# Issuing all q and k transposes of a group ahead of their two PSUM copies, and loading the first V later, in a chunked attention followed by a squared-ReLU FFN

## The chip, the cores and the metric

The kernel runs on one NeuronCore of a Trainium2 chip. TensorE multiplies and transposes into PSUM, VectorE and ScalarE empty PSUM and do the elementwise work, GpSimd casts the weights to bf16, and SyncE issues every transfer between HBM and SBUF, in the order of the program. The metric is the device time of one execution in microseconds, lower being better.

## What is computed

Attention within chunks of 64 positions, over 8 batches, 8 heads, 576 positions and a head dimension of 64, and then a two-layer FFN over the 4608 tokens.

```python
scores = scale * np.matmul(q_c, k_c.transpose(0, 1, 2, 4, 3))    # per chunk of 64
attn = np.exp(scores - max)
attn = attn / (np.sum(attn, axis=-1, keepdims=True) + 1e-09)
x = np.matmul(attn, v_c)              # -> tokens x 512
h = np.maximum(x @ w_in, 0.0)         # 512 -> 2048
out = h * h @ w_out                   # 2048 -> 512
```

## The kernel before

The 4608 tokens are cut into 18 groups of 256 (two tiles of 128 tokens, `t` or `i` in the code), and the groups into blocks: groups 0 to 2, then seven pairs (3 and 4, up to 15 and 16), and group 17 alone. A block is the unit of the FFN; the attention of the next block's groups is woven into it.

The attention of a group has four steps. `transpose_qk` (T, line 129) takes the upper bf16 half of the fp32 q and k tiles and transposes them on TensorE, 8 transposes of 128 x 128 for q and 8 for k (line 139). They go into one PSUM tile `ps_att` of two banks, q in the first and k in the second. VectorE copies the q half to the SBUF tile `qkT` (line 146), ScalarE the k half (line 148). In the program the q transposes come first, then the q copy, then the k transposes, then the k copy. `scores` (SC, line 150) multiplies the chunks from `qkT` into another `ps_att` tile, and ScalarE takes the exponential (line 167). `values` (AV, line 170) multiplies with V, which has a column of ones that gives the sums, and VectorE divides (lines 186 and 189). `transpose_x` (XT, line 195) transposes the result into `xT`, with a copy on VectorE (line 209). `ps_att` has two buffers for all these steps.

The FFN of a block goes in slots. A slot of `ffn_in` (line 217) is one of 16 columns of tiles: 4 matmuls into a `ps_ffn` buffer (line 224), a relu on ScalarE (line 230) and a square on VectorE (line 231). A slot of `ffn_out` (line 235) is 4 of the 16 matmuls of an output tile (line 240); behind the last of them stand ScalarE's copy to `o_sb` (line 247, four buffers) and the store (line 249). `ps_ffn` has four buffers, so that slot n of `ffn_in` needs the buffer that the relu of slot n - 4 (or an output copy) has read.

The order is written out by hand (`manual_schedule`): each engine works through its instructions in the order of the program. The steps T, SC, AV, XT of groups 0 and 1 run ahead of everything, one after the other. In block 0, T of group 2 stands behind slot 3, and those of groups 3 and 4 behind slots 44 and 46, in its `ffn_out`. In the blocks that follow, T of the next pair stands behind slots 1 and 4 of `ffn_in`, the scores of both behind slot 9, the values behind 14 and 18, the last transposes behind 22 and 26.

The loads are issued by SyncE in a fixed order: q,k and then V of group 0, the same of group 1, two of the eight pieces of w_in (256 columns each, cast by GpSimd at line 113, each good for two slots), group 2, the other pieces of w_in, w_out, and the groups of the next two blocks; later ones at the start of each block, ahead of the stores of that block. `load_qk` (line 77) issues 4 transfers, or more where a batch ends within the group; `load_v` (line 90) issues 6 or more, as V is stored with its odd heads in swapped chunks.

Of the kernel before, what the change touches and what calls it, by code (L numbers as in the profile page):

```python
# [10 lines left out]
BF16 = mybir.dt.bfloat16  # L11
# [5 lines left out]
def kernel(  # L17
# [16 lines left out]
    n_hp = H // 2  # L34
    n_dt = d_model // 128
    n_ft = d_ff // 128
    GT = 256
# [8 lines left out]
    att_pool = ctx.enter_context(tc.tile_pool(name="att", bufs=3))  # L46
# [20 lines left out]
    def segments(g0, n):  # L67
        while n:
            b, s = divmod(g0, S)
            m = min(n, S - s)  # L70
            yield b, s, m
            g0 += m
            n -= m
# [3 lines left out]
    def load_qk(g):  # L77
        q_sb = in_pool.tile([128, 2, H, D], FP32, name="q_sb")
        k_sb = in_pool.tile([128, 2, H, D], FP32, name="k_sb")
        qk[g] = (q_sb, k_sb)  # L80
        for t in range(2):
            for dst, src in ((q_sb, q), (k_sb, k)):
                p = 0
                for b, s, m in segments(g * GT + t * 128, 128):
                    nc.sync.dma_start(  # L85
                        out=dst[p:p + m, t, :, :],
                        in_=src[b, :, s:s + m, :].rearrange("h s d -> s h d"))
                    p += m

    def load_v(g):  # L90

        vt = v_tiles[g % NV]
        for t in range(2):
            g0 = g * GT + t * 128
            p = 0
            for b, s, m in segments(g0, 128):
                nc.sync.dma_start(  # L97
                    out=vt[p:p + m, t, 0::2, 0:D],
                    in_=v[b, 0::2, s:s + m, :].rearrange("h s d -> s h d"))
                p += m  # L100
            for half in range(2):
                b, s = divmod(g0 + 64 * half, S)
                p = 64 * (1 - half)
                nc.sync.dma_start(  # L104
                    out=vt[p:p + 64, t, 1::2, 0:D],
                    in_=v[b, 1::2, s:s + 64, :].rearrange("h s d -> s h d"))

    def load_w_in(i):
        cols = slice(i * 256, (i + 1) * 256)
        st = wst_pool.tile([128, 1024], FP32, name="w_st").rearrange("p (a f) -> p a f", a=n_dt)  # L110
        nc.sync.dma_start(  # L111
            out=st, in_=moe_w_in[:, cols].rearrange("(a p) f -> p a f", p=128))
        nc.gpsimd.tensor_copy(out=w_in_bf[:, :, cols], in_=st)  # L113
# [15 lines left out]
    def transpose_qk(g):  # L129
        ps = ps_att.tile([128, 1024], FP32, name="ps_att")  # L130
        psb = ps.bitcast(BF16)
        qkT = att_pool.tile([128, 2, n_hp, GT], BF16, name="qkT")
        state["qkT", g] = qkT
        for which in range(2):
            srcb = qk[g][which].bitcast(BF16)
            for hp in range(n_hp):
                for i in range(2):
                    c0 = which * 1024 + hp * GT + i * 128
                    nc.tensor.transpose(  # L139
                        out=psb[:, c0:c0 + 128],  # L140
                        in_=srcb[:, i, 2 * hp:2 * hp + 2, 1::2],
                        identity=ident)
            dst = qkT[:, which]
            src = psb[:, which * 1024:(which + 1) * 1024].rearrange("c (h t) -> c h t", h=n_hp)
            if which == 0:
                nc.vector.tensor_copy(out=dst, in_=src)  # L146
            else:
                nc.scalar.copy(out=dst, in_=src)  # L148

    def scores(g):  # L150
        qkT = state.pop(("qkT", g))
        ps = ps_att.tile([128, 1024], FP32, name="ps_att")
        for hp in range(n_hp):
            for t in range(2):
                for a in range(2):
                    for p in range(2):
                        c = p ^ a
                        cols = slice(t * 128 + p * 64, t * 128 + p * 64 + 64)
                        o0 = a * 512 + hp * 128 + t * 64
                        nc.tensor.matmul(  # L160
                            out=ps[64 * c:64 * c + 64, o0:o0 + 64],
                            lhsT=qkT[64 * a:64 * a + 64, 1, hp, cols],
                            rhs=qkT[64 * a:64 * a + 64, 0, hp, cols],
                            start=True, stop=True)
        e = att_pool.tile([128, 2, n_hp, 2, 64], BF16, name="e")
        state["e", g] = e
        nc.scalar.activation(  # L167
            out=e.rearrange("p a h t q -> p (a h t q)"), in_=ps, func=AF.Exp, scale=scale)
# [26 lines left out]
    def transpose_x(g):  # L195
# [5 lines left out]
        for t in range(2):  # L201
# [9 lines left out]
            in_=psb[:, 0:1024].rearrange("p (h t) -> p h t", h=n_hp))  # L211

    T, SC, AV, XT = transpose_qk, scores, values, transpose_x

    gTs = {}
# [37 lines left out]
    def load(g):  # L253
        load_qk(g)
        load_v(g)

    load(0)
    load(1)
    load_w_in(0)
    load_w_in(1)  # L260
    load(2)
    for i in range(2, 8):
# [10 lines left out]
    for j, grps in enumerate(blocks):  # L273
# [4 lines left out]
        if j == 0:  # L278
            a, b = nxt
# [4 lines left out]
        else:  # L284
            if len(nxt) == 2:
                a, b = nxt
                plan = {1: [(T, a)], 4: [(T, b)], 9: [(SC, a), (SC, b)], 14: [(AV, a)],
                        18: [(AV, b)], 22: [(XT, a)], 26: [(XT, b)]}
            elif nxt:
                a, = nxt  # L290
# [40 lines left out]
```

## Time and profile before

| | us |
|---|---|
| time, median of 3 runs | 353.45 (352.02 to 353.71) |
| the profiled execution, its own time | 352.24 |
| its span, from the first to the last instruction | 350.2 |
| TensorE busy, of the span | 303.3 |
| TensorE's wait in the middle of T, all groups | 23.9 |
| VectorE, ScalarE, GpSimd busy | 120.7, 142.7, 18.6 |

The profile is that of one execution. A page sums up each engine's busy time; views of the trace list the waits of each engine with what ended them, the instructions in order of time, the chain of work that ended last, and the busy time by stretch. L139 is line 139 of the kernel before. PE is TensorE, PEld its weight load, DVE VectorE, ACT ScalarE, POOL GpSimd, SPq the queue from which SyncE issues transfers.

### The profile page before, as it was taken

How to read it: one execution, taken by the hardware profiler on the slowest of the kernel's cores; microseconds unless marked ns; L12 is line 12 of the kernel's file. 1: busy time of each engine (PE TensorE's matmuls, PEld its weight loads, DVE VectorE, ACT ScalarE, POOL GpSimd, SP SyncE). 2: the span in 40 equal slices, each digit the busy share in tenths (PEclk: the TensorE clock that was granted, in tenths of full speed). 3: DMA queues.
4: the chain of work that ended last, by engine and by line, in shares of the span. 5: the costliest groups of instructions: out<-in, count | busy, mean ns of one | idle time of the engine just before them, and what ended most of it. 6: DMA issues, size and time to landing. Idle time of an engine off the chain costs nothing.

```text
span 350.2 us, 6792 instructions
## 1 busy us (share of the span) xinstructions
PE 303.3 (87%) x2800; PEld 157.9 (45%) x2800; DVE 120.7 (34%) x268; ACT 142.7 (41%) x233; POOL 18.6 (5%) x28
## 2 busy tenths in 40 slices
PE   2456979989589988998899889988998899899995
PEld 1322447444244544454445444544454445444472
DVE  0322395015235314531453145314531453144050
ACT  0323545250455146514651465146514651473171
POOL 1021681000000000000000000000000000000000
PEclk9999899999699999999999999999999999999999
DMA  9997998998992159414861586159615601100101
GB/s 168 193 229 217 366 362 179 200 172 172 278 187 48 60 140 199 85 62 117 183 122 62 135 168 121 63 136 171 115 62 138 104 2 60 62 0 31 60 32 60
DMA packets 125278, 46.58 MB, mean 133 GB/s; under 512 B 114496, under 2 KB 118592, under 8 KB 125248
## 3 DMA queue, kind: packets, MB, share of 16 engines
q1 hardware_dynamic: 125248, 46.15, 56.9%
q8 instruction: 22, 0.36, 0.5%
q14 instruction: 8, 0.07, 0.1%
HBM read 36.70 MB, written 9.44 MB: 132 GB/s over the span
## 4 chain that ended last, share of the span: by engine, by line
PE 78%; SPq 8%; DVE 6%; ACT 3%; DMA 2%; issue 1%; POOL 0%; ACTq 0%
PE ps_ffn L240 36%; PE ps_ffn L224 35%; SPq L85 3%; PE ps_att L139 3%; DVE gT L231 3%; DVE qkT L146 3%; ACT rl L230 3%; SPq L104 2%; PE ps_att L205 2%; SPq L97 2%; PE ps_att L179 2%; PE ps_att L160 2%; DMA w_st<-in_moe_w_in_dram 1%; DMA out_dram<-o_sb 1%; SPq L111 1%
## 5 line engine op out<-in xcount | busy, mean ns | idle before, releaser
L224 PE MATMUL ps_ffn<-xT,w_in_bf 128*128 128x512 bf16 (+1 forms) x640 | 137.5, 369 | 6.1 <-DVE xT L209 4.0
L240 PE MATMUL ps_ffn<-w_out_bf,gT 128*128 128x512 bf16 x576 | 130.0, 379 | 0.0
L231 DVE TENSOR_TENSOR gT<-rl 128x512 bf16<-128x512 bf16 (+1 forms) x160 | 68.0, 428 | 136.2 <-ACT rl L230 131.6
L230 ACT ACTIVATE rl<-ps_ffn 128x512 bf16<-128x512 f32 (+1 forms) x160 | 87.5, 557 | 45.2 <-PE ps_ffn L224 42.7
L224 PEld LDWEIGHTS <-w_in_bf 128*128 128x128 bf16 x640 | 62.0, 100 | 66.1 <-issue 8.8
L240 PEld LDWEIGHTS <-gT 128*128 128x128 bf16 x576 | 55.0, 98 | 62.0
L247 ACT COPY o_sb<-ps_ffn 128x512 f32<-128x512 f32 x36 | 21.1, 586 | 113.4 <-PE ps_ffn L240 103.7
L139 PE MATMUL ps_att<-ident,k_sb 128*128 128x128 bf16 x144 | 12.2, 233 | 23.9 <-DVE qkT L146 23.9
L148 ACT COPY qkT<-ps_att 128x1024 bf16<-128x1024 bf16 x18 | 18.2, 1012 | 35.5 <-PE ps_att L139 35.5
L209 DVE COPY xT<-ps_att 128x1024 bf16<-128x1024 bf16 x18 | 12.4, 691 | 38.7 <-PE ps_att L205 38.7
L189 DVE TENSOR_TENSOR x<-ps_att,rec 128x512 bf16<-128x512 f32 x36 | 24.9, 692 | 1.2
L139 PEld LDWEIGHTS <-k_sb 128*128 128x128 bf16 x144 | 10.5, 104 | 26.3 <-issue 15.7
L146 DVE COPY qkT<-ps_att 128x1024 bf16<-128x1024 bf16 x18 | 12.3, 686 | 21.4 <-PE ps_att L139 21.4
L167 ACT ACTIVATE e<-ps_att 128x1024 bf16<-128x1024 f32 x18 | 17.6, 1023 | 2.1 <-PE ps_att L160 2.1
L139 PE MATMUL ps_att<-ident,q_sb 128*128 128x128 bf16 x144 | 12.0, 229 | 6.2 <-DMA q_sb<-in_q_dram 6.2
L139 PEld LDWEIGHTS <-q_sb 128*128 128x128 bf16 x144 | 10.2, 103 | 10.3 <-DMA q_sb<-in_q_dram 6.3
L186 DVE RECIPROCAL rec<-ps_att 128x8 f32<-128x8 f32 x36 | 7.2, 201 | 22.0 <-PE ps_att L179 22.0
L205 PE MATMUL ps_att<-ident,x 128*128 128x128 bf16 x144 | 12.2, 229 | 2.2 <-DVE x L189 2.2
L205 PEld LDWEIGHTS <-x 128*128 128x128 bf16 x144 | 9.9, 101 | 6.8 <-DVE x L189 3.0
L179 PEld LDWEIGHTS <-e 64*64 64x64 bf16 x576 | 6.5, 111 | 9.3 <-issue 5.5
L179 PE MATMUL ps_att<-v_sb,e 64*64 64x65 bf16 x576 | 8.6, 200 | 2.3 <-ACT e L167 2.3
L113 POOL CAST w_in_bf<-w_st 128x1024 bf16<-128x1024 f32 x8 | 8.8, 1096 | 32.7 <-DMA w_st<-in_moe_w_in_dram 32.7
(12 smaller groups left out, 24.6 us busy)
## 6 DMA issues: line engine op xcount, KB each, us to landing
out_dram<-o_sb SPq DMA_DIRECT2D x36, 256.0 KB, 2.0
q_sb<-in_q_dram SPq DMA_DIRECT2D x32, 256.0 KB, 4.3
k_sb<-in_k_dram SPq DMA_DIRECT2D x32, 256.0 KB, 4.8
v_sb<-in_v_dram SPq DMA_DIRECT2D x80, 64.0 KB, 3.0
v_sb<-in_v_dram SPq DMA_DIRECT2D x32, 128.0 KB, 4.5
w_st<-in_moe_w_in_dram SPq DMA_DIRECT2D x8, 512.0 KB, 5.7
w_st<-in_moe_w_out_dram SPq DMA_DIRECT2D x8, 512.0 KB, 6.3
q_sb<-in_q_dram SPq DMA_DIRECT2D x8, 128.0 KB, 3.6
```

Of the source, the lines that this page charges most:

```text
L139: nc.tensor.transpose(out=psb[:, c0:c0 + 128], in_=srcb[:, i, 2 * hp:2 * hp + 2, 1::2], identity=ident)
L146: nc.vector.tensor_copy(out=dst, in_=src)
L148: nc.scalar.copy(out=dst, in_=src)
L167: nc.scalar.activation(out=e.rearrange("p a h t q -> p (a h t q)"), in_=ps, func=AF.Exp, scale=scale)
L179: nc.tensor.matmul(out=ps[64 * p:64 * p + 64, a, hp * (D + 1):(hp + 1) * (D + 1)], lhsT=e[64 * c:64 * c + 64, a, hp, t, :], rhs=vb[64 * c: ...
L189: nc.vector.tensor_tensor(out=x.rearrange("p h a d -> p a h d"), in0=o[:, :, :, 0:D], in1=rec.to_broadcast([128, 2, n_hp, D]), op=ALU.mult)
L205: nc.tensor.transpose(out=psb[:, c0:c0 + 128], in_=x[:, hp].rearrange("p a d -> p (a d)"), identity=ident)
L224: nc.tensor.matmul(out=h[:, 0:n], lhsT=w_in_bf[:, dt, ft * 128:(ft + 1) * 128], rhs=xT[:, dt, c:c + n], start=(dt == 0), stop=(dt == n_dt ...
L230: nc.scalar.activation(out=rl[:, 0:n], in_=h[:, 0:n], func=AF.Relu)
L231: nc.vector.tensor_tensor(out=gT[:, ft, c:c + n], in0=rl[:, 0:n], in1=rl[:, 0:n], op=ALU.mult)
L240: nc.tensor.matmul(out=o_ps, lhsT=gT[:, ft, tt * 128:(tt + 1) * 128], rhs=w_out_bf[:, ft, :], start=(ft == 0), stop=(ft == n_ft - 1))
L247: nc.scalar.copy(out=o_sb, in_=o_ps)
```

## The change

All 16 transposes of a group are issued first, q and then k, and the two copies after them. Within each half the PSUM columns and the `qkT` tile are ordered by token tile first and head pair second, instead of the other way round, and the scores' slices follow; every run that an instruction reads or writes stays 64, 128 or 1024 elements long. In the loads, q,k of groups 0 and 1 come first, then V of group 0, w_in 0, V of group 1, w_in 1; from group 2 on the order is the same as before.

```diff
@@ transpose_qk
-        qkT = att_pool.tile([128, 2, n_hp, GT], BF16, name="qkT")
+        qkT = att_pool.tile([128, 2, 2, n_hp, 128], BF16, name="qkT")
         state["qkT", g] = qkT
         for which in range(2):
             srcb = qk[g][which].bitcast(BF16)
             for hp in range(n_hp):
                 for i in range(2):
-                    c0 = which * 1024 + hp * GT + i * 128
+                    c0 = which * 1024 + i * 512 + hp * 128
                     nc.tensor.transpose(
                         out=psb[:, c0:c0 + 128],
                         in_=srcb[:, i, 2 * hp:2 * hp + 2, 1::2],
                         identity=ident)
-            dst = qkT[:, which]
-            src = psb[:, which * 1024:(which + 1) * 1024].rearrange("c (h t) -> c h t", h=n_hp)
+        for which in range(2):
+            dst = qkT[:, which].rearrange("c t h q -> c (t h q)")
+            src = psb[:, which * 1024:(which + 1) * 1024]
             if which == 0:
                 nc.vector.tensor_copy(out=dst, in_=src)
             else:
@@ scores
-                        cols = slice(t * 128 + p * 64, t * 128 + p * 64 + 64)
+                        cols = slice(p * 64, p * 64 + 64)
...
-                            lhsT=qkT[64 * a:64 * a + 64, 1, hp, cols],
-                            rhs=qkT[64 * a:64 * a + 64, 0, hp, cols],
+                            lhsT=qkT[64 * a:64 * a + 64, 1, t, hp, cols],
+                            rhs=qkT[64 * a:64 * a + 64, 0, t, hp, cols],
@@ loads
-    load(0)
-    load(1)
+    load_qk(0)
+    load_qk(1)
+    load_v(0)
     load_w_in(0)
+    load_v(1)
     load_w_in(1)
     load(2)
```

## Rows read from the trace of the kernel before

**Rows 1.** The page, busy time of each engine, share of the span, instructions.

```profile
PE 303.3 (87%) x2800; PEld 157.9 (45%) x2800; DVE 120.7 (34%) x268; ACT 142.7 (41%) x233; POOL 18.6 (5%) x28
```

**Rows 2.** The waits: who waited for whom, us in total, times, longest.

```profile
PE ps_att L139 <- DVE qkT L146: 23.9, 18, 3.5
```

**Rows 3.** Stretches: us, busy time by engine, PEclk, DMA share, GB/s; a steady block.

```profile
126.03:161.05 35.02, 32.36 (x306) 16.32 (x304) 12.62 (x28) 15.29 (x24) 0.00 (x0) 1.00 0.57 121
```

**Rows 4.** Timeline of a steady block: start, duration, instruction, [idle before <- releaser].

```profile
197.62 0.61 PE L139 MATMUL ps_att<-ident,q_sb 128*128 128x128 bf16 x8
...
198.79 0.68 DVE L146 COPY qkT<-ps_att 128x1024 bf16<-128x1024 bf16 x1
...
199.53 0.61 PE L139 MATMUL ps_att<-ident,k_sb 128*128 128x128 bf16 x8 [1.30 <-DVE qkT L146]
...
200.17 1.01 ACT L148 COPY qkT<-ps_att 128x1024 bf16<-128x1024 bf16 x1 [1.76 <-PE ps_att L139]
...
204.53 0.61 PE L139 MATMUL ps_att<-ident,k_sb 128*128 128x128 bf16 x8 [1.36 <-DVE qkT L146]
...
209.39 0.71 PE L160 MATMUL ps_att<-qkT 64*64 64x64 bf16 x64
```

**Rows 5.** Timeline from the end of block 0 into block 1.

```profile
70.44 0.61 PE L139 MATMUL ps_att<-ident,k_sb 128*128 128x128 bf16 x8 [0.78 <-DVE qkT L146]
...
85.71 4.20 SPq L249 DMA_DIRECT2D out_dram<-o_sb  x6
...
88.17 0.59 ACT L247 COPY o_sb<-ps_ffn 128x512 f32<-128x512 f32 x1 [9.46 <-PE ps_att L139]
88.97 0.59 ACT L247 COPY o_sb<-ps_ffn 128x512 f32<-128x512 f32 x1 [0.21 <-DMA out_dram<-o_sb]
...
91.65 1.01 PE L139 MATMUL ps_att<-ident,k_sb 128*128 128x128 bf16 x8 [3.54 <-DVE qkT L146]
...
92.46 5.18 PE L224 MATMUL ps_ffn<-xT,w_in_bf 128*128 128x512 bf16 x12
...
104.35 0.71 PE L160 MATMUL ps_att<-qkT 64*64 64x64 bf16 x64
...
106.76 1.63 ACT L230 ACTIVATE rl<-ps_ffn 128x512 bf16<-128x512 f32 x3
```

**Rows 6.** Timeline of the start: loads, groups 0 to 2, the first FFN slots.

```profile
3.73 1.08 SPq L97 DMA_DIRECT2D v_sb<-in_v_dram  x1
...
10.67 0.93 SPq L85 DMA_DIRECT2D k_sb<-in_k_dram  x1
...
12.31 0.66 PE L179 MATMUL ps_att<-v_sb,e 64*64 64x65 bf16 x32 [1.13 <-ACT e L167]
...
24.57 5.83 PE L224 MATMUL ps_ffn<-xT,w_in_bf 128*128 128x512 bf16 x16 [0.78 <-DVE xT L209]
...
33.74 1.04 POOL L113 CAST w_in_bf<-w_st 128x1024 bf16<-128x1024 f32 x1 [9.24 <-DMA w_st<-in_moe_w_in_dram]
...
34.84 4.27 PE L224 MATMUL ps_ffn<-xT,w_in_bf 128*128 128x512 bf16 x12 [2.07 <-POOL w_in_bf L113]
```

**Rows 7.** The k copy's line: ScalarE's queue, ns min/median/max, first and last start.

```profile
L148 ACTq EVENT_SEMAPHORE  x18: 17/17/17, 8.1 to 304.6; - x18
```

**Rows 8.** Timeline of group 17, the last q copy.

```profile
303.87 0.68 DVE L146 COPY qkT<-ps_att 128x1024 bf16<-128x1024 bf16 x1
```

**Rows 9.** The chain of work that ended last: start, us, engine, tile, line.

```profile
69.21 0.46 PE ps_att L139 x8
...
135.12 4.32 PE ps_ffn L224 x20
```

**Rows 10.** Stretches with the granted clock (the third column from the end).

```profile
90.50:91.00 0.50, 0.00 (x0) 0.00 (x0) 0.44 (x3) 0.04 (x1) 0.00 (x0) 0.54 1.07 320
...
47.50:51.00 3.50, 1.08 (x7) 0.36 (x5) 3.50 (x5) 1.20 (x2) 3.02 (x3) 1.00 1.02 378
```

**Rows 11.** Issues of V's line 104 up to 36 us.

```profile
DMA to landing us min/median/max: 2.7/3.6/4.5
```

## The prediction

> **What bounds the kernel now.** I read the page's busy shares first: TensorE is busy 87% of the span and no other engine over 45% [rows 1], so what matters is where TensorE stands still. The view of waits puts the largest sum of its waits on line 139: 23.9 us in 18 waits for VectorE's copy of line 146, one for each group [rows 2]. The table by stretches then shows how much that is of a steady block of two groups: 35.02 us, of which TensorE is busy 32.36 [rows 3]. The timeline of such a block has the missing 2.66 us as two gaps and nothing else: the 8 q transposes end, TensorE waits 1.30 us (in the block's second group 1.36) until the q copy is done, and only then come the 8 k transposes [rows 4]. The 18 waits are 0.78 us in groups 0, 1, 3 and 4 (one row stands for them), 1.30 in group 2, 3.54 in group 5, 1.36 in group 6, 1.30 and 1.36 in the five pairs of groups 7 to 16, and 1.30 in group 17; together 23.9 [rows 2, 4, 5].
>
> Before about 92 us the bound is another one. The chip's transfers run almost without a pause from the start, and TensorE meets two gates that SyncE's queue sets: the third piece of w_in, whose cast ends at 34.78, with the matmuls that need it at 34.84 [rows 6], and the first two stores of the output, issued from 85.71 on, behind every load of groups 3 to 6; ScalarE's copies of the fifth and sixth output tile (there are four o_sb buffers) wait for them until 88.17 and 88.97 [rows 5]. What TensorE wins ahead of a gate is lost at it.
>
> **The change part by part.**
>
> *Transposes ahead of the copies.* Same 16 transposes, same two copies, same bytes; the four edits of layout only reorder columns in runs that stay contiguous, so I cost them at nothing (copies of 0.68 and 1.01 us either way [rows 4]). What goes is TensorE's wait between the two halves. What is late next? The ScalarE queue has a semaphore step ahead of each of the 18 k copies, the first at 8.1 and the last at 304.6, when the last q copy (303.87, 0.68 long) has just ended; so the k copy waits for the q copy [rows 7, 8]. I take that to stay. Then the relus of the next slots, queued on ScalarE behind the k copy, hold ps_ffn buffers that TensorE wants four slots later. Worked through in a steady block: a slot is 4 matmuls of 0.216 (20 in 4.32) = 0.86 us, 16 transposes are twice 0.46 = 0.9 us, a relu is 0.54 us in a row of them (3 in 1.63) [rows 4, 5, 9]. T of the first group runs 197.62 to 198.52. The q copy starts at 198.79 as before (VectorE is busy until then), ends 199.47; the k copy runs 199.55 to 200.5, relus of slots 2 to 4 follow. T of the second group: 201.10 to 202.00; its q copy stands behind the square of slot 4 and ends at 203.23, the k copy at 204.22; the relu of slot 5 ends at 204.82. TensorE reaches slot 9, which needs that buffer, at 205.45: 0.63 us to spare. The scores come at 206.3 with the k copy two microseconds old, against 209.39 before; the k copy's own two releases of the rotating ps_att buffers are as early. So nothing takes the wait's place, and a steady block gains 2.66 us: five blocks 13.3 us, group 17 another 1.3. Behind the waiting k copy stand only relus; behind the q copy, which now waits for the k transposes too, only squares, and it was not ready to start sooner.
>
> *Groups 0 to 4.* In groups 0 and 1 nothing else is at hand for TensorE, and the chain transposes, q copy, k copy, scores keeps its length: 0 us. Group 2's 1.30 us ends at the gate of 34.84: 0. The 0.78 us of groups 3 and 4 bring TensorE to block 1 1.56 us sooner, and the gate of the stores takes it: 0.
>
> *Groups 5 and 6.* Here the old wait was 3.54 us because the q copy stood behind squares, relus and the two output copies that the stores held. After: slots 0 and 1 and all 16 transposes end at about 87 (91.65 less 3.54 is 88.11; less 1.56, plus 0.45 for the k half); slot 2 needs the buffer that the output copy at 88.17 (0.59 long) frees, so it starts at 88.82 instead of 92.46. The clock decides the rest. Before, it was granted 0.54 in the half microsecond from 90.5, after 2.4 us of standing still, and the 12 matmuls that began at 92.46 took 5.18 us instead of 2.6 [rows 5, 10]. Now the idle stretch is about 1.9 us; one of 2.4 us before 50.83 passed at full clock [rows 10]. At full clock slots 2 to 4, T of group 6 and slots 5 to 8 end at 95.8, slot 9 waits 1.1 us for ScalarE (relus 2 to 4 and the k copies start late here), and the scores come at 97.8 instead of 104.35: 6.5 us won, of which 4.9 are the old waits. With a fall to half clock it is some 4.5 to 5. I take 6.0, nearer the row that held its clock.
>
> *V behind q,k.* No transfer is added. In SyncE's queue the 6 of V of group 0 move behind 4 of group 1's q,k, and V of group 1 behind w_in 0, whose cast comes sooner on an idle GpSimd. All the bytes of the two groups are then issued by the same time as before, so w_in 2 and everything later keeps its time. But V of group 0 was issued from 3.73; now its last piece takes the place that the last k of group 1 had, 10.67 to 11.6 [rows 6], or about 12 since six short issues cost more than the rate of the transfers. With 2.7 to 3.6 us to landing [rows 11] it is there at 14.3 to 15.6. The values matmuls ran at 12.31 [rows 6], so they start 2 to 3.3 us late (q,k half of that chain is late too: the q copy now waits for the k data and the table load comes after it). TensorE takes groups in order, so the first FFN matmul, 24.57, goes to about 27.3. Its 16 matmuls took 5.83 us (33.1), T of group 2 one (34.1): still ahead of 34.84, by 0.7 us. Cost 0, ends 0 and +2.
>
> The Trainium skill speaks against this part: "DMA: Bandwidth & Descriptors", Rules for kernel authors, wants a transfer issued early and waited for late. By that rule the 3 us would stand in the result (334.6); the trace's gate at 34.84 says they don't.
>
> **Sum.** 13.3 + 1.3 + 6.0 = 20.6 us off the profiled execution's own 352.24 (span 350.2 and 2.04 around it, unchanged): 331.6. That execution lies near the low end of the three runs, whose median is 353.45, so I add 0.4: **332.0 us**.
>
> **Rivals.**
> 1. *ScalarE holds the buffers.* The margin of 0.63 us at slot 9 is thin. If the two copies, now behind each other with no wait of TensorE beside them, cost twice as long, the relu of slot 5 is 1.7 us late and TensorE waits 1.1 us in each of 7 blocks: about 339. For it: in block 1 it happens by my own working. Against: the copies' durations hardly vary.
> 2. *V leaks through.* With the slow clock through slots 0 to 3 (0.43 us a matmul, 6.8 us) the gate of 34.84 is passed 1 to 2 us late; the stores' gate still has 1.9 us to absorb it. Only the rest counts: up to 334.
> 3. *Slower: the clock falls at each T.* If 16 transposes in a row let the clock drop to 1.2 GHz as after group 5, each fall costs some 2.6 us (5.18 against 2.6); one a block eats the gain, two a block cost 2.6 more than that: 352.2 + 5 x 2.6 + 1.3 - 5 = 361.5. It decides from one fall a block. Against: before, each T had 0.45 + 1.30 + 0.45 us without FFN matmuls and the clock stood at 1.00 all through [rows 3, 4]; now there are 0.9. The Trainium skill, "TensorE: Matmul & The Clock Gate", Part 4: PE-mode transpose, says that the full clock doesn't engage for transposes; by that rule alone this rival would come about, and the steady 1.00 of the row does not bear it out.
> 4. *The wait stays*, because the k transposes wait for something else that ends with the q copy: 352. Against: the gap ends with that copy 18 times of 18.
>
> **How the numbers follow.** Forecast 0.75 (330 to 334.5), rival 1 0.12 (335 to 340), rival 2 0.08 (333 to 335), rival 3 0.02, rival 4 0.03. Range 329.5 to 337.5: it takes in both clocks of block 1, V's leak and half of rival 1. Half a per cent (1.8 us) is about what a measurement of this kernel can tell from no change: faster 0.95, same 0.03, slower 0.02.
>
> **What would show it.** Line 139 has no more waits for line 146; the steady block is 32.4 us with TensorE never idle; k copies start 0.1 us after q copies end; slot 9 waits nowhere but in block 1; the third w_in cast still ends near 34.8 and the first store goes out near 85.7; FFN starts near 27; slot 2 of block 1 starts near 88.8. I am wrong if steady blocks stay over 33 us, if the first store moves, or if a drop of the granted clock appears behind a T.

## The result and the profile after

| | before | after |
|---|---|---|
| time, median of 4 runs | 352.96 (352.02 to 353.71) | 329.5 (328.88 to 331.99) |
| the profiled execution, its own time | 352.24 | 328.88 |
| its span | 350.2 | 327.1 |
| TensorE's wait for the q copy in T | 23.9 | 0 |

The ratio is 0.935 (0.9293 to 0.9406): 6.5% faster. All times are in microseconds. In the changed kernel the lines behind 144 have moved by one: 147 is the q copy, 149 the k copy, 161 the scores, 225 and 241 the FFN's matmuls, 248 and 250 the output's copy and store.

A steady block of the changed kernel, which answers to [rows 3]; the columns are those of rows 3:

```profile
119.36:151.40 32.04, 31.78 (x301) 16.25 (x304) 12.62 (x28) 14.85 (x24) 0.00 (x0) 1.00 0.61 132
```

The block went from 35.02 to 32.04. Its timeline, which answers to [rows 4]:

```profile
120.92 0.61 PE L139 MATMUL ps_att<-ident,q_sb 128*128 128x128 bf16 x8
121.37 0.61 PE L139 MATMUL ps_att<-ident,k_sb 128*128 128x128 bf16 x8
121.82 2.54 PE L225 MATMUL ps_ffn<-xT,w_in_bf 128*128 128x512 bf16 x11
...
122.10 0.68 DVE L147 COPY qkT<-ps_att 128x1024 bf16<-128x1024 bf16 x1
122.81 1.01 ACT L149 COPY qkT<-ps_att 128x1024 bf16<-128x1024 bf16 x1 [1.09 <-DVE qkT L147]
...
125.68 0.68 DVE L147 COPY qkT<-ps_att 128x1024 bf16<-128x1024 bf16 x1
126.40 1.01 ACT L149 COPY qkT<-ps_att 128x1024 bf16<-128x1024 bf16 x1 [1.09 <-DVE qkT L147]
...
129.71 0.71 PE L161 MATMUL ps_att<-qkT 64*64 64x64 bf16 x64
```

In the block no TensorE row carries an idle time in brackets (x301 against x306: some matmul records are missing). The 16 transposes run from 120.92 to 121.82, the FFN goes straight on, and the k copy starts 0.03 after the q copy ends. From T to the scores it is 8.79 (129.71 - 120.92); before it was 11.77 [rows 4].

The start, which answers to [rows 6]:

```profile
0.74 1.28 ACT L149 ACT_TABLE_LOAD   x1 [0.74 <-PEq L318]
...
13.74 0.42 PE L180 MATMUL ps_att<-v_sb,e 64*64 64x65 bf16 x3 [2.29 <-DMA v_sb<-in_v_dram]
...
14.38 1.29 PE L180 MATMUL ps_att<-v_sb,e 64*64 64x65 bf16 x29 [0.21 <-DMA v_sb<-in_v_dram]
...
26.25 0.58 PE L225 MATMUL ps_ffn<-xT,w_in_bf 128*128 128x512 bf16 x1 [0.78 <-DVE xT L210]
...
32.89 1.04 POOL L113 CAST w_in_bf<-w_st 128x1024 bf16<-128x1024 f32 x1 [8.86 <-DMA w_st<-in_moe_w_in_dram]
...
33.99 1.90 PE L225 MATMUL ps_ffn<-xT,w_in_bf 128*128 128x512 bf16 x8 [1.76 <-POOL w_in_bf L113]
```

V of group 0 now holds TensorE up (2.29), the FFN starts 1.7 later than before (26.25 against 24.57), and TensorE still waits 1.76 for the third piece of w_in, whose cast ends at 33.93 (before 34.78): V's delay has ended at that gate. Behind it the matmuls ran at full clock (8 recorded in 1.90), where before 12 took 4.27 [rows 6]. A third wait, which the prediction does not name, stands between the two gates: at slot 16 TensorE waits 2.29 for VectorE's copy of xT (2.42 before). The copy stands behind four squares that take 3.68 there, 0.92 each, while GpSimd casts pieces of w_out; a square of the same size takes 0.43 in a steady block, where GpSimd does nothing. No run takes the casts away, so that they are the reason is not shown.

The way into block 1, which answers to [rows 5]:

```profile
85.65 4.21 SPq L250 DMA_DIRECT2D out_dram<-o_sb  x6
85.69 0.61 PE L139 MATMUL ps_att<-ident,k_sb 128*128 128x128 bf16 x8
...
88.14 0.59 ACT L248 COPY o_sb<-ps_ffn 128x512 f32<-128x512 f32 x1 [11.69 <-DMA out_dram<-o_sb]
88.78 2.75 PE L225 MATMUL ps_ffn<-xT,w_in_bf 128*128 128x512 bf16 x11 [2.48 <-ACT o_sb L248]
...
96.72 1.02 PE L225 MATMUL ps_ffn<-xT,w_in_bf 128*128 128x512 bf16 x4 [0.83 <-ACT rl L231]
...
97.68 0.71 PE L161 MATMUL ps_att<-qkT 64*64 64x64 bf16 x64
```

The first store goes out at 85.65 as before (85.71), and TensorE now stands still behind it, before slot 2, instead of inside T. The matmuls from 88.78 run at full clock (11 of the 12 recorded, 2.75), where before 12 took 5.18. Slot 9 waits 0.83. The scores come at 97.68 instead of 104.35.

So the 23.36 of the two profiled executions are made up of 6.67 up to the scores of groups 5 and 6 (104.35 - 97.68), 14.93 from there to the scores of groups 15 and 16 (five blocks, 2.97 to 3.02 each), 1.50 in the rest (70.74 against 69.24), and 0.26 around the span.

### The profile page after: what moved, and what is told of

The parts are those of the page before. It is cut to its first block, busy times and chain, and to the rows that moved or that the text cites. A ratio compares the mean times of both kernels' runs of the same rounds, so it can differ in the third digit from the quotient of the medians.

```text
span 327.1 us, 6732 instructions
## 1 busy us (share of the span) xinstructions
PE 295.6 (90%) x2758; PEld 156.8 (48%) x2800; DVE 121.8 (37%) x268; ACT 139.4 (43%) x233; POOL 18.6 (6%) x28
## 4 chain that ended last, share of the span: by engine, by line
PE 81%; SPq 8%; DMA 4%; DVE 3%; issue 2%; ACT 1%; POOL 0%; ACTq 0%
PE ps_ffn L241 38%; PE ps_ffn L225 34%; PE ps_att L139 4%; SPq L85 4%; SPq L104 2%; PE ps_att L206 2%; DMA w_st<-in_moe_w_in_dram 2%; PE ps_att L180 2%; PE ps_att L161 2%; SPq L97 2%; DVE gT L232 2%; DMA k_sb<-in_k_dram 1%; ACT rl L231 1%; DMA out_dram<-o_sb 1%; SPq L111 1%
## 5 line engine op out<-in xcount | busy, mean ns | idle before, releaser
L225 PE MATMUL ps_ffn<-xT,w_in_bf 128*128 128x512 bf16 (+1 forms) x616 | 132.4, 363 | 10.6 <-DVE xT L210 3.9
L241 PE MATMUL ps_ffn<-w_out_bf,gT 128*128 128x512 bf16 x558 | 128.5, 379 | 1.1 <-issue 0.3
L232 DVE TENSOR_TENSOR gT<-rl 128x512 bf16<-128x512 bf16 (+1 forms) x160 | 68.9, 434 | 112.3 <-ACT rl L231 106.0
L231 ACT ACTIVATE rl<-ps_ffn 128x512 bf16<-128x512 f32 (+1 forms) x160 | 84.8, 561 | 33.1 <-PE ps_ffn L225 30.3
L180 PE MATMUL ps_att<-v_sb,e 64*64 64x65 bf16 x576 | 9.5, 200 | 3.8 <-DMA v_sb<-in_v_dram 2.5
L161 PE MATMUL ps_att<-qkT 64*64 64x64 bf16 x576 | 7.0, 197 | 3.7 <-ACT qkT L149 3.7
```

Of the source, the lines that this page charges most:

```text
L161: nc.tensor.matmul(out=ps[64 * c:64 * c + 64, o0:o0 + 64], lhsT=qkT[64 * a:64 * a + 64, 1, t, hp, cols], rhs=qkT[64 * a:64 * a + 64, 0, t, ...
L180: nc.tensor.matmul(out=ps[64 * p:64 * p + 64, a, hp * (D + 1):(hp + 1) * (D + 1)], lhsT=e[64 * c:64 * c + 64, a, hp, t, :], rhs=vb[64 * c: ...
L225: nc.tensor.matmul(out=h[:, 0:n], lhsT=w_in_bf[:, dt, ft * 128:(ft + 1) * 128], rhs=xT[:, dt, c:c + n], start=(dt == 0), stop=(dt == n_dt ...
L231: nc.scalar.activation(out=rl[:, 0:n], in_=h[:, 0:n], func=AF.Relu)
L232: nc.vector.tensor_tensor(out=gT[:, ft, c:c + n], in0=rl[:, 0:n], in1=rl[:, 0:n], op=ALU.mult)
L241: nc.tensor.matmul(out=o_ps, lhsT=gT[:, ft, tt * 128:(tt + 1) * 128], rhs=w_out_bf[:, ft, :], start=(ft == 0), stop=(ft == n_ft - 1))
```

## The experiments

The theory: all of the gain is TensorE's wait in T; what comes ahead of two gates (the third piece of w_in, the first stores) counts for nothing; V and the layout count for nothing; the k copy waits for the q copy. The rivals are in the expectations. Ratios are to the kernel before on the same chip.

**The order alone.** In the kernel before, the two copies go into a loop of their own behind all 16 transposes; layout and loads stay:

```diff
                         identity=ident)
+        for which in range(2):
             dst = qkT[:, which]
...
```

> The kernel before with nothing changed but the order: 16 transposes, then the two copies; old layout of qkT, old order of the loads. Theory (all of the gain is TensorE's wait in T, the layout and V cost and give nothing): 329.5 us, 329 to 331, a steady block of two groups 32.04 us. Rival A (V behind q,k gives part of it, as the changed kernel passes the third piece of w_in 0.85 us and reaches block 1 2.3 us sooner): 331 to 333. Rival B (the layout gives the 0.33 us by which a steady block gained more than the 2.66 us that the waits sum to): steady block 32.36 us, 331 us.

Measured: 330.55, ratio 0.9374 (0.9317 to 0.9431). The scores in its timeline:

```profile
131.56 0.71 PE L161 MATMUL ps_att<-qkT 64*64 64x64 bf16 x64
...
163.60 0.71 PE L161 MATMUL ps_att<-qkT 64*64 64x64 bf16 x64
```

They are 32.04 apart, as in the changed kernel, so the layout gives nothing in a steady block and rival B falls. The whole time can't be told from the changed kernel's; rival A's 331 to 333 overlaps with the interval, and the next run bears on it.

**V alone.** The kernel before with the loads of the change:

```diff
-    load(0)
-    load(1)
+    load_qk(0)
+    load_qk(1)
+    load_v(0)
     load_w_in(0)
+    load_v(1)
     load_w_in(1)
```

> The kernel before with nothing changed but the loads: q,k of groups 0 and 1 first, then V of 0, w_in 0, V of 1, w_in 1. Theory (the gates of w_in and of the first stores hide the start): first FFN matmul 2 to 3 us later, time as before, 353 us within 1. Rival A: 350 to 352. Rival C (V's delay comes through): 355 to 356.

Measured: 352.31, ratio 1.0021 (0.9981 to 1.0062): no difference that can be measured. Against the 353 of the expectations rival A (0.992 to 0.997) lies outside, and rival C's 355 (1.006) only just inside. Its profiled execution, one of the two slowest of 12 (354.92):

```profile
27.21 0.59 PE L224 MATMUL ps_ffn<-xT,w_in_bf 128*128 128x512 bf16 x1 [0.78 <-DVE xT L209]
...
35.73 2.76 PE L224 MATMUL ps_ffn<-xT,w_in_bf 128*128 128x512 bf16 x12 [0.67 <-POOL w_in_bf L113]
...
89.32 4.29 SPq L249 DMA_DIRECT2D out_dram<-o_sb  x6
...
95.36 1.01 PE L139 MATMUL ps_att<-ident,k_sb 128*128 128x128 bf16 x8 [5.05 <-DVE qkT L146]
```

The FFN starts 2.6 later than in the kernel before and still waits 0.67 for w_in. The first store went out 3.6 later here, and the wait in group 5 grew with it (5.05 against 3.54): the k transposes come 6.04 behind the store, before 5.94 [rows 5].

**The old order for groups 0 to 4.** In the changed kernel:

```diff
...
+        steps = (transposes, copy, transposes, copy) if g < 5 else (transposes, transposes, copy, copy)
...
```

> The changed kernel with the old order (q transposes, q copy, k transposes, k copy) for groups 0 to 4 alone. Theory of the gates: what these groups win is lost at the first store, so the time is that of the changed kernel, 329.5 us within 1; TensorE reaches block 1 about 2 us later and waits there for ScalarE's output copy as much less. Rival (each wait counts where it stands): 3 x 1.46 us for groups 2 to 4 and some 0.5 for 0 and 1 come back, 334 us.

Measured: 331.15, ratio 0.94 (0.9357 to 0.9444). 334 would be 0.949 and lies outside, so the rival falls. The median is 1.65 above the changed kernel's, outside the expected "within 1", though the intervals of the two ratios overlap. The five waits that are back in T sum to 4.4, and TensorE stands 4.11 at the gate:

```profile
87.09 4.40 SPq L255 DMA_DIRECT2D out_dram<-o_sb  x6
...
90.39 4.44 PE L230 MATMUL ps_ffn<-xT,w_in_bf 128*128 128x512 bf16 x11 [4.11 <-ACT o_sb L253]
```

It was expected to wait about 2 less there than the changed kernel, and waits more: group 5's transposes end at 86.28, as in the changed kernel (86.30), which had lost 1.67 to a slow clock on the way (below), and the store goes out later. Behind the 4.11 the clock was granted at half (0.50 from 92 to 94), so that 11 matmuls took 4.44.

The gate shows best when profiles with the new order in group 5 and four `o_sb` buffers are laid side by side. TensorE is done with group 5's transposes at different times, but slot 2 starts 3.1 to 3.4 behind the first store in each of them:

| kernel | transposes of group 5 end | first store | slot 2 | slot 2 behind the store |
|---|---|---|---|---|
| changed | 86.30 | 85.65 | 88.78 | 3.13 |
| order alone | 85.21 | 86.97 | 90.15 | 3.18 |
| old order to group 4 | 86.28 | 87.09 | 90.39 | 3.30 |
| two SBUF tiles (below) | 84.77 | 86.58 | 89.96 | 3.38 |
| k copy twice (below) | 87.50 | 84.33 | 87.52 | 3.19 |

(In the last, TensorE itself was as late as the gate, so that this row does not test it. With two PSUM tiles, below, the k transposes of group 5 are what needs the buffer: they start 3.14 behind the store, at 89.42, after a wait of 2.35.)

**Does the k copy wait because of the SBUF tile?** q and k halves of `qkT` in two tiles:

```diff
-        qkT = att_pool.tile([128, 2, 2, n_hp, 128], BF16, name="qkT")
+        qkT = [att_pool.tile([128, 2, n_hp, 128], BF16, name=n) for n in ("qT", "kT")]
...
```

> The changed kernel with the q and k halves of qkT in two SBUF tiles of their own. Theory (the k copy waits for the q copy because both write one SBUF tile): the two copies start together, in block 1 the k copies come 1 us sooner and the 0.83 us wait at slot 9 goes, elsewhere TensorE has no wait to lose: 328.7 us (328 to 329.5). Rival (the wait comes from the shared PSUM tile): the k copy still starts 0.1 us after the q copy ends, 329.5 us.

Measured: 330.52, ratio 0.9406 (0.9369 to 0.9443). ScalarE's waits (line, releaser, sum, times, longest):

```profile
ACT kT L149 <- DVE qT L147: 33.8, 18, 7.5
```

All 18 k copies still wait for the q copy, so the theory of this run fell. Then the PSUM tile was split as well, the k transposes going to a buffer of `ps_ffn`:

```diff
+        psb = [ps_att.tile([128, 1024], FP32, name="ps_att").bitcast(BF16),
+               ps_ffn.tile([128, 512], FP32, name="ps_ffn").bitcast(BF16)]
...
```

> The changed kernel with two SBUF tiles for q and k, and with the k transposes in a PSUM tile of their own, taken from the rotation of ps_ffn (one of its four buffers for a short while). Theory (the k copy waits for the q copy because both read one PSUM tile): in the steady blocks the k copy starts ahead of the q copy, right behind the transposes and the relu before it, and nothing of ScalarE's waits names the q copy any more; the time stays near that of the changed kernel, 329 to 332 us, or up to 335 where the borrowed buffer is missed. Rival (some other order between the two engines): the k copy still starts 0.05 us after the q copy ends.

Measured: 330.13 in two runs, ratio 0.9362 (0.9218 to 0.9507). A steady block of it:

```profile
122.34 1.01 ACT L149 COPY kT<-ps_ffn 128x1024 bf16<-128x1024 bf16 x1 [0.30 <-PE ps_ffn L139]
122.42 0.68 DVE L147 COPY qT<-ps_att 128x1024 bf16<-128x1024 bf16 x1
```

Now the two run side by side, and no wait of ScalarE names the q copy any more. So the shared PSUM tile is enough to put one copy behind the other, though they read different banks of it. No gain in time shows, as in the steady blocks TensorE has no wait there to lose; with two runs and a borrowed buffer the interval is wide.

**How much room has ScalarE?** The k copy issued twice:

```diff
                 nc.scalar.copy(out=dst, in_=src)
+                nc.scalar.copy(out=dst, in_=src)
```

> The changed kernel with ScalarE's k copy issued twice (0.92 us more on ScalarE for each group). Theory of the four ps_ffn buffers: in a steady block the relu of slot 5 then ends 1.8 us later, and TensorE, with 0.6 us to spare, waits 1.2 us at slot 9; with 1.8 us more in block 1 and nothing in group 17 and the start: 337 us (335 to 339). Rival (the relus behind the k copy have room for it): 329.5 to 331 us, no wait at slot 9.

Measured: 339.05, ratio 0.9624 (0.9574 to 0.9674). TensorE's waits, and slot 9 in a steady block:

```profile
PE ps_ffn L226 <- ACT rl L232: 8.4, 7, 1.9
...
130.90 1.02 PE L226 MATMUL ps_ffn<-xT,w_in_bf 128*128 128x512 bf16 x4 [1.13 <-ACT rl L232]
```

The wait appears where the four buffers put it, with 1.13 where 1.2 was worked out. The scores of steady blocks are 33.33 apart, 1.29 more than the 32.04 of the changed kernel: again 0.16 more than the idle row says (see the point on a steady block's gain below). The whole time rose more than the expected 337; its median lies at the upper end of the 335 to 339.

**Taking the second gate away.** Six `o_sb` buffers, so that no output copy of block 0 waits for a store, in the changed kernel and in the kernel before:

```diff
-                    o_sb = ffn_pool.tile([128, d_model], FP32, name="o_sb", bufs=4)
+                    o_sb = ffn_pool.tile([128, d_model], FP32, name="o_sb", bufs=6)
```

> The changed kernel with six o_sb buffers instead of four, so that no output copy of block 0 waits for a store. Theory of the second gate: TensorE's 2.48 us wait for the output copy at 88.8 and the 0.83 us at slot 9 of block 1 go: 326.2 us (325.5 to 327.5). Rival (the transfers hold block 1 by something else, such as V of group 6, issued until 85.6): 328.5 to 329.5 us.

> The kernel before with six o_sb buffers. Theory: group 5's wait shrinks from 3.54 to the 1.3 us of the other groups (2.2 us) and, if the clock holds there, the 2.6 us of slow matmuls behind it go too: 348 to 351 us. Rival (the wait of 3.54 us has nothing to do with the stores): 353 us within 1.

Measured: the changed kernel 323.34, ratio 0.9201 (0.9166 to 0.9237); the kernel before 347.97, ratio 0.9902 (0.9867 to 0.9938). The changed kernel with six:

```profile
84.93 2.75 PE L225 MATMUL ps_ffn<-xT,w_in_bf 128*128 128x512 bf16 x12
86.71 4.21 SPq L250 DMA_DIRECT2D out_dram<-o_sb  x6
...
92.83 0.71 PE L161 MATMUL ps_att<-qkT 64*64 64x64 bf16 x64
```

Slot 2 starts 1.8 ahead of the first store, without a wait, and the scores come 4.85 sooner. The medians are 6.2 apart, 3 more than the 3.3 that I read from the changed kernel's profile. Of the 4.85 between the two profiles 3.3 are those two waits, and most of the rest is that group 5's transposes end 1.2 sooner (85.09 against 86.30), without the slow clock that the changed kernel's execution had from 49.5 on. The last 1.3 is that this execution was the fastest of its kernel's runs and the profiled one with six buffers the slowest of six. It is the fastest version found. The kernel before gains 3.4 from the six buffers by its ratio (2.2 to 4.7). In the profile group 5 waits 1.36 instead of 3.54, and the 12 matmuls behind it take 2.75 instead of 5.18, together 4.6; 4.0 of it is there at the scores (100.33 against 104.35), as TensorE came to group 5 some 1.0 later, its clock having fallen to half earlier, behind the wait at slot 16.

> The changed kernel with two SBUF tiles for q and k and six o_sb buffers. Theory: as with six o_sb buffers alone, as the slot 9 wait is already gone there: 326 us (325 to 327.5). Rival: the two gains add, 325 us or less.

With two SBUF tiles and six buffers: 324.4, ratio 0.9248 (0.9201 to 0.9295), not faster than six buffers alone: the rival's 325 or less is met only because those came to 323.34, and its sum of two gains is not there.

**V and groups 0 to 4 again, without the second gate.** On one chip, six buffers each: the changed kernel, the same with V's old place, the same with the old order to group 4.

> The changed kernel with six o_sb buffers (which take away the gate of the first stores) and the old order of the loads, V of groups 0 and 1 straight behind their q,k. Theory (V's delay ends at the third piece of w_in, not only at the stores): the same as six o_sb buffers with the changed loads, within 0.7 us. Rival A (the changed order of the loads gains at the start): 0.8 to 2 us slower. Rival C (V's delay comes through once the second gate is gone): 0.8 to 2 us faster.

> The changed kernel with six o_sb buffers and the old order of transposes and copies for groups 0 to 4. Theory of the gates: without the gate of the stores the old waits of groups 3 and 4 come back (0.78 us and 0.16 for the drained TensorE each, 1.9 us), that of group 2 still ends at w_in: 1.9 us slower than six o_sb buffers alone (1.3 to 2.5). Rival (what these groups win is lost somewhere else than at the stores): within 0.7 us of it.

> The changed kernel with six o_sb buffers once more, on the chip of the two others: the measure for both. 323.3 us, 322.5 to 324.5.

Measured: 324.95, ratio 0.9226 (0.9189 to 0.9263), with V's old place; 327.11, ratio 0.929 (0.9255 to 0.9325), with the old order to group 4; 323.73, ratio 0.9192 (0.9161 to 0.9222), for the repeat. V's new place is not slower: rival C falls. Its median is 1.2 better, more than the 0.7 of the theory and within rival A; the intervals overlap, so a gain of about 1 stays open. The profiles do not show it: with the old place TensorE waits 3.30 for the third piece of w_in and runs behind it at half clock (0.50 from 36 to 38; the order alone 3.19 and half clock too), with the new one it waits 0.66 in the repeat and keeps full clock. But slot 16 starts at 49.73 and 49.21 with the old place, and at 48.68 to 51.67 in the seven profiles with the new place and the new order.

The old order costs 3.4 here, where with the gate it could not be told apart. Its profile, and behind it that of the repeat, with the waits of T's line 139 and of slot 16:

```profile
35.55 0.61 PE L139 MATMUL ps_att<-ident,k_sb 128*128 128x128 bf16 x8 [1.62 <-DVE qkT L148]
35.99 2.75 PE L230 MATMUL ps_ffn<-xT,w_in_bf 128*128 128x512 bf16 x12
...
50.01 7.16 PE L230 MATMUL ps_ffn<-xT,w_in_bf 128*128 128x256 bf16 x64 [2.08 <-DVE xT L215]
...
75.45 0.71 PE L166 MATMUL ps_att<-qkT 64*64 64x64 bf16 x64
```

```profile
34.56 2.76 PE L225 MATMUL ps_ffn<-xT,w_in_bf 128*128 128x512 bf16 x12 [0.66 <-POOL w_in_bf L113]
...
50.33 7.16 PE L225 MATMUL ps_ffn<-xT,w_in_bf 128*128 128x256 bf16 x64 [2.66 <-DVE xT L210]
...
73.88 0.71 PE L161 MATMUL ps_att<-qkT 64*64 64x64 bf16 x64
```

From slot 16 to the scores of groups 3 and 4 it is 25.44 and 23.55: the 1.89 between them is what was worked out for the waits of these two groups, and now that the stores hold nothing back it stays (scores of groups 5 and 6 at 95.48 and 93.91). So what groups 3 and 4 win was indeed lost at the stores. At the first gate the old order is 1.4 later (35.99 against 34.56), but at slot 16 it is not (50.01 against 50.33): that lateness is gone there. The two profiled executions are 1.57 apart, the medians 3.4; what the other 1.8 are is open.

## Why the prediction was right, point by point

- *The bound.* Right for the steady blocks: the wait of line 139 is gone and nothing took its place; the profile has TensorE without a gap there. Ahead of 92 us I named two gates and left out the wait at slot 16.
- *The size of a steady block's gain.* Mis-sized: 2.98 instead of 2.66. I counted the wait as the view of waits has it, from the end of the last q transpose to the first k transpose. But T took 2.35 in all before (197.62 to the FFN's next matmul at 199.97) and takes 0.90 now (120.92 to 121.82), which is 1.45 and not 1.30: transposes start every 0.056 but each lasts 0.22, so that a wait also lets the last one run out (0.16). The order alone, with the old layout, has the same 32.04, so it isn't the layout; and a wait of 1.13 in the kernel with the k copy twice cost 1.29. Over groups 7 to 16 the term is 14.9 where I had 13.3, and 1.50 for group 17 and the tail where I had 1.3.
- *Groups 5 and 6.* Right in the mechanism and nearly to the tenth: slot 2 at 88.78 (88.82 was worked out), the wait at slot 9 of 0.83 (1.1), the scores at 97.68 (97.8). I took 6.0 of the 6.5 at full clock; it was 6.67. My reason for the clock was weak, though. I judged by a wait of 2.4 that had passed at full clock; in the changed kernel one of 2.29 before 48.78 was followed by a fall to 1.2 GHz, here in the timeline and in a stretch of half a microsecond (granted clock third from the end; 0.50 from 50 to 53),

```profile
48.78 8.83 PE L225 MATMUL ps_ffn<-xT,w_in_bf 128*128 128x256 bf16 x64 [2.29 <-DVE xT L210]
```

```profile
49.50:50.00 0.50, 0.50 (x5) 0.39 (x4) 0.16 (x1) 0.45 (x2) 0.50 (x1) 0.74 1.05 385
```

  and the one of 2.48 before 88.78 was not. The 64 matmuls from 48.78 took 8.83 instead of 7.16; the second gate swallowed that. That the clock held at 88.78 is luck in part: in the three like it, where the store came later and the wait was 4.11 to 5.19, the clock fell to half, and the scores came at 99.44 (order alone), 99.97 and 100.39, 4.0 to 4.9 sooner than before. That is about the 4.5 to 5 of the prediction's other branch.
- *Groups 0 to 4 and V at nothing.* Right within what the runs can tell. The gate of the stores was shown by taking it away; that of w_in only by TensorE's waits there (1.76; 0.67 with V alone), as no run takes it away. The first FFN matmul was put at 27.3 and came at 26.25. I had ScalarE's table load behind the q copy, but it ran at 0.74, so the first k copy was done about 1.3 sooner than I had it; that gained nothing, as the values of group 0 then waited 2.29 for V. The last piece of V that they waited for was there at 14.38, at the early end of my 14.3 to 15.6, so that T of group 1 came 2.07 late (17.16 against 15.09), and group 1's chain from T to the values was 0.4 shorter than before (5.33 against 5.73), where I had it unchanged.
- *The k copy waits for the q copy.* Right (18 of 18), and harmless as worked out; its cause is the shared PSUM tile.
- *Rival 1* (ScalarE holds the buffers) did not come about, but the room is as thin as stated: 0.92 more on ScalarE for each group brings 8.4 of waits and 339.05 in place of 329.5, the prediction's "about 339". *Rival 2*: no leak of V can be measured (0.9981 to 1.0062 with V alone). *Rival 3*: the granted clock is 1.00 in all steady blocks, so 16 transposes in a row did not lower it; the rule in the Trainium skill, "TensorE: Matmul & The Clock Gate", Part 4: PE-mode transpose, had no such effect here. *Rival 4* is out.
- *The sum.* For the profiled execution 331.6 was worked out and 328.88 measured: 1.8 of the difference are the transposes that run out, 0.7 groups 5 and 6, and 0.26 lies around the span. I added 0.4 for the median, 332.0; it was 0.6, 329.5. The median lies on the range's lower bound, below the 330 to 334.5 that had the chance of 0.75, and two of the four runs lie below the range: that it was reached at all is luck. What I left out of its lower end was a wait's true cost being larger than its idle row.

## What to carry to other kernels

When one engine fills a buffer in halves and two others empty them, issue all the filling first: the waits that go are worth more than their idle rows, by the time the pipelined instructions take to run out (0.16 for each wait here). Before costing a gain, look for the next gate behind it: here what groups 2 to 4 win ended at two gates that SyncE's queue sets, and the cheapest next step was two more output buffers. One profile shows one case of a gate whose time varies; several profiles laid side by side show the gate itself.

## What the runs showed of the hardware that I had not expected

- The first store, at the end of a fixed row of loads, went out between 84.33 and 89.32 in the profiles of these kernels, though the loads behind group 1 are the same; in two executions of one kernel (six buffers) it was 86.71 and 88.00. With four `o_sb` buffers slot 2 follows it; with six it doesn't.
- The wait at slot 16 stands in all 14 profiles, and the 64 matmuls behind it show the clock. In four it fell to half (granted 0.50; waits of 2.29, 2.44, 2.47 and 2.55; the matmuls took 8.78 to 8.83), in ten it stayed at full (waits of 1.72 to 2.66; 7.16 to 7.24). The length of a wait alone does not decide, and a forecast there has to carry both.
- Two copies from different banks of one PSUM tile to two SBUF tiles ran one behind the other on VectorE and ScalarE, and side by side from two PSUM tiles. A semaphore step of the program stands ahead of each k copy [rows 7], so this is how the program orders them; what the two banks would allow without it, no run shows.
